# M5 of the last pass at the second level of Strassen-Winograd, with sums on VectorE and two fixed staging slots

## The chip, the cores and the metric

The kernel runs on one core of a Trainium2 chip. The metric is the device time of one execution in microseconds (us); lower is better. Engines that matter here: TensorE (PE in the profile; its weight loads are PEld), VectorE (DVE), ScalarE (ACT), GpSimd (POOL) and SyncE (SP), whose queue issues most of the transfers between the chip's main memory (DRAM) and the on-chip SBUF. Products accumulate in PSUM, eight banks of 512 fp32 columns.

## The reference, cut to what matters

```python
xn = layernorm(x)                               # x: 2048 x 1024
s  = linear_attention(xn, wqkv, 32 heads) @ wo
b  = (silu(xn @ w_gate) * (xn @ w_up)) @ w_down # 1024 -> 3584 -> 1024
out = x + s * silu(b)
```

Weights and activations are bf16. The change concerns the last of these products, `h @ w_down`, for the second half of the tokens that is worked on, and the write-out behind it.

## The kernel before, in words

The feed-forward part works in two passes of 1024 tokens. A pass first makes `h = silu(gate) * up`, [1024 x 3584] kept with the 3584 on partitions as 28 chunks of 128, in 28 steps (one weight block of gate or of up each), and then multiplies by `w_down`. Every product uses the Strassen-Winograd scheme: the operands are cut into 2x2 quarters, and seven products of quarters take the place of eight, with sums of quarters made before and after. For `h @ w_down` the quarters of `h` are A11, A12, A21, A22 (512 tokens x 14 chunks each); the products are M1 = A11 B11, M2 = A12 B21, M7 = S3 T3, M6 = S2 T2, M5 = S1 T1, M4 = A22 T4, M3 = S4 B22, in this order (`M_ORDER`), with S1 = A21+A22, S2 = S1-A11, S3 = A11-A21, S4 = A12-S2. M5 needs S1, written in place of A21.

In the last pass (`emit_down_m`, L1394) such a product is either done directly (`prod_t`, L1433: four token tiles, each 14 matmuls of 128x512), or cut once more by the same scheme ("second level", `l2_M`, L1469). The second level needs seven products of halves of tokens, chunks and columns: for each of two row halves 7 matmuls of 128x256. `L2 = (1, 2, 4)` says that M1, M2 and M4 are done so. It costs three kinds of preparation:

- *Sums of weights.* `l2_load` (L1102) loads a piece of the packed `w_down` from the DRAM tensors `wd`, `l2_sums` (L1134) makes four differences on GpSimd (L1144) and stores seven blocks to the DRAM tensor `l2_M` (L1145). This is done for M1 and M4 during the 28 steps of the last pass, in pieces of two chunk pairs (the fourth piece of each M is half as large): a load in every odd step (L1737), the differences a step later. M2's sums are made earlier by another way. Later `load_w` (L238) loads them from there.
- *Sums of activations* s1 to s4 (`l2_lhs`, L1160), chunk pair by chunk pair on GpSimd, 28 operations of 128x256 for each M. For M1 they lie in two slots of the weight ring (`r_spare`), for M2 and M4 in old tiles (`x_spare`).
- *Sums of results* on VectorE and ScalarE, in `l2_M`, with steps that let one M's products run while another's results are copied: a `yield` after the first two products, and a call of `fill()` ahead of product 4.

The weight ring (`w_slot`, L215) has 8 slots of 1 MB. All weights of the steps (`pk_g`, `pk_u`: one block a step), the staging pieces, `r_spare` and the weights of M1 to M3 go through it. `load_w_to(base + i + 5)` (L1697) asks for the block of step i+4, so five steps ahead at most. SyncE issues its transfers in an order that a planner lays down when the program is built; each transfer waits in that queue for what it needs (a free slot, a finished store), and what is queued behind it waits too. The order on the other four engines is the order of the program.

A step of the pass is `emit_a` of the next block (four products of 4 matmuls, L988 to L991) and `emit_b` of the current one (three, L1017 to L1019). 28 matmuls, all L966.

The write-out of a tile of results is `fin` (L1196): `y*s` (L1200), plus `x` (L1201), and a store (L1202). Its `x` and `s` come by `io_load` (L1184), one tile ahead of need in a pool `io` of five slots; the last three of the kernel go to the tiles S0, S1, S2 of the pool `sp`, which hold the sums of the activations of the gate and up products until the last `emit_a`. `k2` are small result tiles; `KA` and `KB` (L1538, L1545) hold running sums of results in fp32; `banks()` hands out four PSUM banks, in turn from two pools.

Of the kernel before, what the change touches and what calls it, by code (L numbers as in the profile page):

```python
# [21 lines left out]
def kernel(  # L22
# [165 lines left out]
    passes = list(range(NPASS - 1, -1, -1))  # L188
    NWA = NFG // 2
    M_ORDER = (1, 2, 7, 6, 5, 4, 3)  # L190
    L2 = (1, 2, 4)
    L2_ORDER = (1, 2, 5, 6, 7, 4, 3)
    NQ = NFG // 2
    CH = CW // 2
# [20 lines left out]
    def w_slot():  # L215
        return wgu.tile([P, 2, DC, FW], BF16, name="w_sb", tag="pk")
# [52 lines left out]
    def load_w_to(n):  # L269
        while w_next[0] < min(n, len(w_seq)):  # L270
            load_w()
# [680 lines left out]
    with ExitStack() as p3:  # L952
# [8 lines left out]
        def k2(shape, dt, name):  # L961
            return kp.tile(shape, dt, name=name, tag="k2")
# [135 lines left out]

        l2_q = deque((M, j) for M in L2 if M != 2 for j in range(0, NQ, 2))
        l2_live = deque()  # L1100

        def l2_load():  # L1102
            M, j0 = l2_q.popleft()
            kd, q = M_PACK[M]
            t = w_slot()
            v = t[:].rearrange("p h a b -> p (h a b)").rearrange("p (b j n) -> p b j n", b=8, n=CH)
            js = range(j0, min(j0 + 2, NQ))
            for j in js:
                for k, b0, b1 in ((0, 0, 7), (1, 1, 6)):
                    src = wd_drams[j][0 if kd == "a" else 1][:, k, q].rearrange("p (c n) -> p c n", n=CH)  # L1110
                    nc.sync.dma_start(out=v[:, b0:b1 + 1:b1 - b0, j - j0, :], in_=src)
            l2_live.append((M, js, v))
# [31 lines left out]
                nc.gpsimd.tensor_tensor(out=b(o_), in0=b(a_), in1=b(b_), op=ALU.subtract)  # L1144
            nc.gpsimd.dma_start(out=l2_drams[M][:, :, js.start:js.stop, :], in_=v[:, 0:7, 0:n_, :])  # L1145

        x_spare, r_spare = [], []

        def l2_bufs(M):
            v = [x[:].rearrange("p a b -> p (a b)").bitcast(F16) for x in x_spare]  # L1150
            if M == 1:
                v = [x[:].rearrange("p h a b -> p (h a b)").bitcast(F16) for x in r_spare]
            v = [x[:, 0:2 * NQ * 2 * P].rearrange("p (s j r n) -> p s j r n", s=2, j=NQ, r=2) for x in v]
            return [v[0][:, 0], v[0][:, 1], v[1][:, 0], v[1][:, 1]]

        def l2_quad(A, j):
            v = A[:, :, j].rearrange("p k (r t n) -> p k r t n", r=2, t=2)
            return v[:, 0, :, 0], v[:, 1, :, 0], v[:, 0, :, 1], v[:, 1, :, 1]

        def l2_lhs(M, A, j, eng):  # L1160
            a11, a12, a21, a22 = l2_quad(A, j)
            s1, s2, s3, s4 = [v[:, j] for v in l2_bufs(M)]
            eng.tensor_tensor(out=s1, in0=a21, in1=a22, op=ALU.add)
            eng.tensor_tensor(out=s2, in0=s1, in1=a11, op=ALU.subtract)
            eng.tensor_tensor(out=s3, in0=a11, in1=a21, op=ALU.subtract)
            eng.tensor_tensor(out=s4, in0=a12, in1=s2, op=ALU.subtract)

        def quads(h, a, t):
            return h[:].rearrange("p (j k a) t -> p k j a t", k=2, a=2)[:, :, :, a, t * TB:(t + 1) * TB]
# [14 lines left out]
        def io_load(after=None):  # L1184
            if not fq:
                return
            p, t, cc = key = fq.pop(0)
            r0 = p * TB2 + t * P
            pool, tg = (sp, "S%d" % len(fq)) if len(fq) < 3 else (iop, "io")
            io = pool.tile([P, 2, CW], BF16, name="io", tag=tg)  # L1190
            gate([nc.sync.dma_start(out=io[:, 0, :], in_=x2[r0:r0 + P, cc * CW:(cc + 1) * CW]),
                  nc.sync.dma_start(out=io[:, 1, :], in_=s_dram[r0:r0 + P, cc * CW:(cc + 1) * CW])],
                 after, sync=True)
            io_tiles[key] = io
# [199 lines left out]
        def emit_down_m(p, h, base):  # L1394
# [8 lines left out]
            def load(M, q=None):  # L1403

                n_ = max(i for i, key in enumerate(seq) if key[2][0] == M and q in (None, key[2][1])) + 1
                load_w_to(base + n_ + (NPK - 2 if M == 1 and q != 3 else NPK))

            def S3(k):
                return s3_[k // NWA][:, k % NWA]
# [7 lines left out]
            def tt(out, a, b_, op=ALU.add):  # L1417
                nc.vector.tensor_tensor(out=out, in0=a, in1=b_, op=op)
# [22 lines left out]
            def banks(n=TPB):  # L1441
                turn[0] += 1
                pool, tg = (pps, "s") if turn[0] % 2 else (ppm, "m")
                return [pool.tile([P, CW], FP32, name="dm", tag=tg)[:] for _ in range(n)]
# [24 lines left out]
            def l2_M(M, A, K, done, fill, in_place, dst=None):  # L1469
# [40 lines left out]
                for r in range(2):  # L1510
                    c0, c1 = c[r]
                    if K is None:
                        nc.scalar.copy(out=c1[:, lo], in_=zy[r][:, lo])
                    else:
                        tt(c1[:, lo], zy[r][:, lo], K[2 * r + 1][:, lo])
                        done(2 * r + 1, c1)
                    l2_p(M, 3, r, A, bk)
                    if in_place:
                        tt(c0, xw[r], K[2 * r])
                    else:  # L1520
                        tt(c0[:, hi], xw[r][:, hi], c0[:, hi])
                    if done is not None:
                        done(2 * r, c0)
# [13 lines left out]
            load_w_to(base + NPK - 2)  # L1537
            KA = kept("kA")  # L1538
            fins = deque()
            M7, M6, M5 = [], [], []  # L1540
            KB = []

            def fill7():
# [17 lines left out]
                flush(1)  # L1561
            load(7)
            sums(S4, A12, S2, ALU.subtract)
            for j in range(NQ):
                l2_lhs(4, quads(h, 1, 1), j, nc.gpsimd)
            M6 = banks()
            for t in range(TPB):
                prod_t(6, t, M6[t], True)
                tt(KB[t], M6[t], KB[t])
                tt(KA[t], M6[t], KA[t])  # L1570
            load(6)
            M5 = banks()
            for t in range(TPB):
                prod_t(5, t, M5[t], True)
                c = k2([P, CW], FP32, "c22")[:]
                tt(c, M5[t], KB[t])
                fins.append((t + TPB, 1, silu(c, "g22")))
                if len(fins) > 1:
                    flush(1)
            tt(KA[-1], M5[-1], KA[-1])  # L1580
            load(5)

            def out3(t):
                prod_t(3, t, M5[t], False)
                c = k2([P, CW], FP32, "c12")[:]
                tt(c, M5[t], KA[t])
                fins.append((t, 1, silu(c, "g12")))

            def done4(t, c):
                fins.append((t + TPB, 0, silu(c, "g21")))  # L1590

            def fill3():
                flush()
                out3(0)
            go(l2_M(4, quads(h, 1, 1), KB, done4, fill3, True))
            hs_ = [slice(0, 3 * CW // 4), slice(3 * CW // 4, CW)]
            out3(1)
            flush(len(fins) - 1)
# [15 lines left out]
        for pi, p in enumerate(passes):  # L1614
# [78 lines left out]
            for i in range(n):  # L1693
# [38 lines left out]
                if not first:  # L1732
                    if l2_live:
                        l2_sums()
                    if i in (17, 18):
                        r_spare.append(w_slot())
                    if i % 2 == 1 and l2_q:  # L1737
                        l2_load()
                    if i >= 18 and 4 * l2_j + 4 <= i:
                        l2_lhs(1, quads(h, 0, 0), l2_j, nc.gpsimd)  # L1740
                        l2_lhs(2, quads(h, 1, 0), l2_j, nc.gpsimd)
                        l2_j += 1
# [41 lines left out]
```

## Time and profile before

| What | us |
|---|---|
| median of 3 runs (lowest, highest) | 756.48 (756.29, 759.92) |
| the profiled execution | 756.18 |
| its span, first to last instruction | 754.4 |
| L966 matmuls of the last pass | to 668.9 |
| M1 begins (L1466) | 668.72 |
| M7, M6 and M5 in a row (L1430) | 693.14 to 726.5 |
| last matmul | 749.8 |
| last write-out addition on VectorE | 751.9 |
| GpSimd: differences for M1 and M4 (L1144), 32 operations | 526.1 to 616.0 |
| GpSimd: sums for M4 (in `l2_lhs`) | 684.4 to 715.5 |

The granted TensorE clock was 0.999 over the span. Times in the profile count from the first instruction. "Busy" is time in which an engine ran an instruction; matmuls overlap in the pipeline, so a single one has a length of 379 ns (width 512) or 273 ns (width 256), though the next starts sooner. The chain that ended last is followed back from the last instruction, at each step to what released it. In the lists of instructions a line has the start, the length, the engine, the line of the kernel, the operation, the tile written and the tile read; `x4` is a group of four.

### The profile page before, as it was taken

To read this page: it belongs to the slowest core of one execution; us is meant where nothing else is said; L and a number is where in the kernel's file an instruction comes from. 1 tells how busy PE (TensorE), PEld (TensorE's weight loads), DVE (VectorE), ACT (ScalarE), POOL (GpSimd) and SP (SyncE) were. 2 spreads that over 40 slices of the span, in tenths; PEclk is the share of its full clock that TensorE was granted. 3 is DMA by queue.
4 is the path that set the end of the run, shared out by engine and by line. 5 is a ranking of instruction groups with operands and counts; after the bars stand their busy time and mean duration, and the time that the engine had idled before them with its cause. 6 is when DMAs were issued, how large, how long until landed. Compare 5 with 4: busy or idle time off the path is not lost.

```text
span 754.4 us, 11075 instructions
## 1 busy us (share of the span) xinstructions
PE 745.8 (99%) x3857; PEld 360.8 (48%) x3857; DVE 581.4 (77%) x1040; ACT 381.1 (51%) x545; POOL 399.8 (53%) x500
## 2 busy tenths in 40 slices
PE   8999999999999999999999999999999999999997
PEld 3544444454454444444444444444444444467464
DVE  6687787887697788888889785468776877687966
ACT  5677776889956575656658311132323222232023
POOL 2444799998540266868585021811542569434900
PEclk9999999999999999999999999999999999999999
DMA  9967799879779668878799228789786768479652
GB/s 318 304 146 139 228 332 298 303 158 271 206 190 296 231 214 301 295 279 316 273 323 409 111 65 306 222 295 339 258 306 222 281 206 344 147 258 318 209 161 77
DMA packets 129160, 187.77 MB, mean 249 GB/s; under 512 B 36208, under 2 KB 104176, under 8 KB 119376
## 3 DMA queue, kind: packets, MB, share of 16 engines
q1 hardware_dynamic: 121760, 156.00, 63.9%
q0 software_dynamic: 5904, 28.58, 9.9%
q10 hardware_dynamic: 1440, 2.49, 1.1%
q8 instruction: 30, 0.49, 0.3%
q14 instruction: 26, 0.21, 0.1%
HBM read 119.47 MB, written 60.23 MB: 238 GB/s over the span
## 4 chain that ended last, share of the span: by engine, by line
PE 84%; DMA 7%; POOL 3%; DVE 2%; issue 2%; ACT 1%; SPq 1%; POOLq 0%; DVEq 0%; ACTq 0%
PE zw L966 19%; PE kv_ps L554 15%; PE xb L966 10%; PE q_ps L183 6%; PE dzw L1228 6%; PE dm L1430 6%; PE yb L966 5%; PE dm L1466 4%; PE dx L1228 3%; DMA l<-w_sb 3%; PE fx L816 3%; DMA w_sb<-wd 3%; PE s_ps L774 3%; POOL w_sb L1144 2%; PE dy L1228 2%
## 5 line engine op out<-in xcount | busy, mean ns | idle before, releaser
L966 PEld LDWEIGHTS <-w_sb 128*128 128x128 f16 (+1 forms) x1568 | 152.1, 98 | 183.8 <-DMA w_sb<-pk_u 1.3
L966 PE MATMUL xb<-xnT,w_sb 128*128 128x512 bf16 x448 | 115.0, 379 | 0.0
L554 PE MATMUL kv_ps<-wkv_sb,xnT 128*128 128x512 bf16 x512 | 113.7, 379 | 0.6 <-ACT xnT L543 0.4
L966 PE MATMUL zw<-xnT,w_sb 128*128 128x512 bf16 x448 | 105.8, 379 | 0.0
L966 PE MATMUL zw<-S,w_sb 128*128 128x512 f16 x448 | 105.8, 379 | 0.0
L321 POOL TENSOR_TENSOR w_sb<-w_sb 128x512 f16<-128x512 bf16 x42 | 50.2, 1195 | 95.7 <-DVE w_sb L309 51.3
L286 ACT ACTIVATE w_sb<-w_sb 128x2048 bf16<-128x2048 bf16 x42 | 79.9, 1902 | 3.9 <-DMA w_sb<-in_B_w_up_dram 3.9
L554 PEld LDWEIGHTS <-xnT 128*128 128x128 bf16 x512 | 48.3, 97 | 56.0 <-ACT xnT L543 0.8
L1144 POOL TENSOR_TENSOR w_sb<-w_sb 128x512 f16<-128x512 bf16 (+3 forms) x32 | 35.4, 1126 | 52.4 <-DMA w_sb<-wd 51.9
L1042 ACT ACTIVATE sg<-cg 128x1024 bf16<-128x1024 f32 x28 | 29.6, 1057 | 57.4 <-DVE cg L1035 57.4
L183 PE MATMUL q_ps<-xnT,wq_sb 128*128 128x512 bf16 x256 | 58.4, 379 | 0.0
L966 PE MATMUL yb<-S,w_sb 128*128 128x512 f16 x224 | 57.4, 379 | 0.8 <-DMA w_sb<-pk_u 0.8
L1035 DVE SCALAR_TENSOR_TENSOR cg<-zw,rc_all,s 128x1024 f32<-128x1024 f32 x28 | 35.9, 1284 | 25.3 <-PE zw L966 13.2
L994 DVE SCALAR_TENSOR_TENSOR s<-yb,rc_all,s 128x512 f32<-128x512 f32 x42 | 31.5, 749 | 27.3 <-ACT s L993 27.3
L322 POOL TENSOR_TENSOR w_sb<-w_sb 128x512 f16<-128x512 bf16 x42 | 50.5, 1202 | 3.3
L324 POOL TENSOR_TENSOR w_sb<-w_sb 128x512 f16<-128x512 bf16 x42 | 50.3, 1197 | 0.0
L323 POOL TENSOR_TENSOR w_sb<-w_sb 128x512 f16<-128x512 bf16 x42 | 50.2, 1196 | 0.0
L1202 POOL DMA_DIRECT2D out_dram<-io x16 | 8.9, 555 | 69.2 <-DVE io L1201 69.0
L993 ACT ACTIVATE s<-xb,rcl 128x512 f32<-128x512 f32 x14 | 9.6, 687 | 66.3 <-PE xb L966 66.3
L1228 PE MATMUL dx<-w_sb,hT 128*128 128x512 bf16 x112 | 42.4, 379 | 0.0
L993 ACT ACTIVATE s<-xb,rc_all 128x512 f32<-128x512 f32 x42 | 28.4, 676 | 22.0 <-issue 12.7
L309 DVE TENSOR_SCALAR w_sb<-w_sb,cs_all 128x2048 bf16<-128x2048 bf16 x35 | 36.7, 1048 | 2.8
(213 smaller groups left out, 1351.1 us busy)
## 6 DMA issues: line engine op xcount, KB each, us to landing
w_sb<-pk_g SPq DMA_DIRECT2D x27, 1024.0 KB, 6.6
pk_g<-w_sb SPq DMA_DIRECT2D x14, 1024.0 KB, 5.0
w_sb<-pk_u SPq DMA_DIRECT2D x14, 1024.0 KB, 8.3
pk_u<-w_sb POOLq DMA_DIRECT2D x13, 1024.0 KB, 5.8
w_sb<-l SPq DMA_DIRECT2D x9, 896.0 KB, 4.6
w_sb<-in_B_w_gate_dram SPq DMA_DIRECT2D x14, 512.0 KB, 6.4
w_sb<-in_B_w_down_dram SPq DMA_DIRECT2D x28, 256.0 KB, 4.8
w_sb<-in_B_w_up_dram SPq DMA_DIRECT2D x14, 512.0 KB, 5.4
```

The source lines that it names most:

```text
L183: nc.tensor.matmul(q_ps[:], lhsT=wq_sb[:, dc, g * P:(g + 1) * P], rhs=xn_ap(dc, btok), start=(dc == 0), stop=(dc == DC - 1))
L286: nc.scalar.activation(out=junk, in_=raw_view(key, t), func=ACT.Square, accum_out=asum[:])
L321: nc.gpsimd.tensor_tensor(out=T1, in0=b12, in1=b11, op=ALU.subtract)
L322: nc.gpsimd.tensor_tensor(out=T2, in0=b22, in1=T1, op=ALU.subtract)
L323: nc.gpsimd.tensor_tensor(out=T3, in0=b22, in1=b12, op=ALU.subtract)
L324: nc.gpsimd.tensor_tensor(out=T4, in0=b21, in1=T2, op=ALU.subtract)
L554: mm = nc.tensor.matmul(kv_ps[:], lhsT=xn_ap(dc, tok), rhs=wkv_sb[:, dc, c * CW:(c + 1) * CW], start=(dc == 0), stop=(dc == DC - 1))
L966: mm = nc.tensor.matmul(out, lhsT=lhs(k), rhs=rhs(k), start=(first and k == 0), stop=(k == HK - 1), skip_group_check=True)
L993: nc.scalar.activation(out=s1[:], in_=x_[:], func=ACT.Copy, scale=rc)
L1144: nc.gpsimd.tensor_tensor(out=b(o_), in0=b(a_), in1=b(b_), op=ALU.subtract)
L1228: nc.tensor.matmul(out, lhsT=lhs, rhs=rhs, start=first, stop=lastk, skip_group_check=True)
L1430: nc.tensor.matmul(out, lhsT=lhs_of(M)(k)[:, t * P:(t + 1) * P], rhs=w_of(M, k)[:, cols], start=first and k == 0, stop=k == NFG - 1, skip_ ...
```

## The change

M5 joins the products of the second level. Its sums of weights are four more staged pieces, so twelve in all. The staging no longer takes a ring slot for each piece: two slots are taken at step 3, and the pieces use them in turn, one piece in each of the steps 3 to 14. The same two slots later hold the sums of activations for M1 and then for M5, so the weights of M1, M2, M7, M6 and of the first three parts of M5 are asked for with six slots in the ring instead of eight. A new function makes the sums of activations for M5 and for M4 on VectorE, in eight operations of 7x128 columns each; for M4 they were 28 operations on GpSimd. M5's results go to fp32 tiles in S0 and S1, and are added from there; M3 gets banks of its own instead of accumulating onto M5's. All io tiles use the `io` pool. M5's first products stand ahead of M4's, and M4's first two fill M5's gap. The diff, cut to its core:

```diff
-    L2 = (1, 2, 4)
+    L2 = (1, 2, 4, 5)
...
         def l2_load():
             M, j0 = l2_q.popleft()
             kd, q = M_PACK[M]
-            t = w_slot()
+            while len(r_spare) < 2:
+                r_spare.append(w_slot())
+            t = r_spare[len(l2_q) % 2]
...
         def l2_bufs(M):
-            if M == 1:
+            if M in (1, 5):
                 v = [x[:].rearrange("p h a b -> p (h a b)").bitcast(F16) for x in r_spare]
...
+        def l2_lhs_all(M, A, eng):
+            sb = l2_bufs(M)
+            for r in range(2):
+                v = A.rearrange("p k j (r t n) -> p k j r t n", r=2, t=2)[:, :, :, r]
+                a11, a12, a21, a22 = v[:, 0, :, 0], v[:, 1, :, 0], v[:, 0, :, 1], v[:, 1, :, 1]
+                s1, s2, s3, s4 = [x[:, :, r] for x in sb]
+                eng.tensor_tensor(out=s1, in0=a21, in1=a22, op=ALU.add)
+                eng.tensor_tensor(out=s2, in0=s1, in1=a11, op=ALU.subtract)
+                eng.tensor_tensor(out=s3, in0=a11, in1=a21, op=ALU.subtract)
+                eng.tensor_tensor(out=s4, in0=a12, in1=s2, op=ALU.subtract)
...
-            pool, tg = (sp, "S%d" % len(fq)) if len(fq) < 3 else (iop, "io")
+            pool, tg = iop, "io"
...
-                load_w_to(base + n_ + (NPK - 2 if M == 1 and q != 3 else NPK))
+                load_w_to(base + n_ + (NPK - 2 if M in (1, 2, 7, 6, 5) and (M, q) != (5, 3) else NPK))
...
             sums(S4, A12, S2, ALU.subtract)
-            for j in range(NQ):
-                l2_lhs(4, quads(h, 1, 1), j, nc.gpsimd)
+            l2_lhs_all(5, quads(h, 0, 1).bitcast(F16), nc.vector)
             M6 = banks()
...
             load(6)
-            M5 = banks()
-            for t in range(TPB):
-                prod_t(5, t, M5[t], True)
-                c = k2([P, CW], FP32, "c22")[:]
-                tt(c, M5[t], KB[t])
-                fins.append((t + TPB, 1, silu(c, "g22")))
-                if len(fins) > 1:
-                    flush(1)
-            tt(KA[-1], M5[-1], KA[-1])
-            load(5)
+            l2_lhs_all(4, quads(h, 1, 1), nc.vector)
+            T5 = [sp.tile([P, 2, CW], FP32, name="kT", tag="S%d" % r) for r in range(2)]
+            T5 = [T5[t // 2][:, t % 2] for t in range(TPB)]
...
-                prod_t(3, t, M5[t], False)
+                prod_t(3, t, M3[t], True)
                 c = k2([P, CW], FP32, "c12")[:]
-                tt(c, M5[t], KA[t])
+                tt(c, M3[t], KA[t])
...
+            def done5(t, T):
+                c = k2([P, CW], FP32, "c22")[:]
+                tt(c, T, KB[t])
+                fins.append((t + TPB, 1, silu(c, "g22")))
+                tt(KA[t], T, KA[t])
+
+            M3 = []
+
             def fill3():
                 flush()
+                M3.extend(banks())
                 out3(0)
-            go(l2_M(4, quads(h, 1, 1), KB, done4, fill3, True))
+            m4_ = l2_M(4, quads(h, 1, 1), KB, done4, fill3, True)
+            go(l2_M(5, quads(h, 0, 1).bitcast(F16), None, done5, lambda: next(m4_), False, T5))
+            go(m4_)
...
-                    if i in (17, 18):
-                        r_spare.append(w_slot())
-                    if i % 2 == 1 and l2_q:
+                    if i >= 3 and l2_q:
                         l2_load()
```

In `l2_M` a call of `done` that stood in one branch now runs whenever `done` is given.

## The prediction

> **What bounds the kernel now.** I read, in this order: the page's busy table, the chain that ended last, the time line of SyncE's queue in the last pass, the waits of that queue, then VectorE's instructions in the last 90 us.
>
> ```profile
> PE 745.8 (99%) x3857; PEld 360.8 (48%) x3857; DVE 581.4 (77%) x1040; ACT 381.1 (51%) x545; POOL 399.8 (53%) x500
> ```
>
> TensorE is the bound: 745.8 of 754.4 us. A change pays only by shortening its stream, or loses by making it wait. The chain of work, around the two places that the change touches:
>
> ```profile
> 604.34 4.67 DMA l<-w_sb
> 609.05 2.17 DMA w_sb<-wd
> 615.04 0.90 POOL l L1145
> 618.67 5.10 DMA w_sb<-pk_u
> 623.81 1.04 PE yb L966 x4
> ...
> 668.88 18.34 PE dm L1466 x168
> 693.30 33.25 PE dm L1430 x154
> ```
>
> (start, length, what). Products of the second level (L1466, 128x256) come every 18.34/168 = 0.1092 us, those of the first (L1430, 128x512) every 33.25/154 = 0.2159. Ahead of them the chain runs through the staging of M1 and M4: a load from wd, four GpSimd differences, a store to `l2_M`, and behind it a weight load that TensorE waits for at 623.81 (the wait table gives that wait 0.8 us). So staging has no slack left even now. SyncE's queue shows why:
>
> ```profile
> 567.81 1.91 SPq L1111 DMA_DIRECT2D w_sb<-wd  x4
> 569.76 0.47 SPq L263 DMA_DIRECT2D w_sb<-pk_g  x1
> 570.27 0.43 SPq L263 DMA_DIRECT2D w_sb<-pk_u  x1
> 581.28 1.91 SPq L1111 DMA_DIRECT2D w_sb<-wd  x4
> 583.23 0.47 SPq L263 DMA_DIRECT2D w_sb<-pk_g  x1
> 583.74 0.43 SPq L263 DMA_DIRECT2D w_sb<-pk_u  x1
> 595.10 1.91 SPq L1111 DMA_DIRECT2D w_sb<-wd  x4
> 609.05 0.88 SPq L1111 DMA_DIRECT2D w_sb<-wd  x2
> ```
>
> ```profile
> SPq L1111 <- DMA l<-w_sb: 47.0, 5, 10.1
> ```
>
> Each staging load waits for the store of the piece before, and the gate/up weights of the next steps stand behind it in the queue. One turn (load, differences, store) takes 13.5, 13.8, 13.95 us.
>
> **Term 1, M5 on TensorE: -1.4.** Out: 4x14 products of 0.2159 = 12.09 us. In: 7 products x 2 row halves x 7 = 98 of 0.1092 = 10.70. All of it is on the path. The Trainium skill (TensorE: Matmul & The Clock Gate, section Back-to-back issue gap) speaks against this: it gives a sustained 131 ns at width 512 and 81 at 128, so by a straight line some 98 ns at 256 (an estimate), and M5 would become 2.3 us longer. This trace has 215.9 and 109.2 ns, and the trace decides.
>
> **Term 2, two waits that go: -0.8 and -0.3.** The 0.8 us at 623 came from slots taken from the ring at steps 17 and 18 just behind the last store; now they are taken at step 3. TensorE also waits 0.28 us at 728.35 for a ScalarE copy behind the g22 silus; in the new order that copy has M5's last products as cover. Bounds: 0 to -1.1.
>
> **Term 3, staging: +2.4 (0 to 9.7).** 12 pieces instead of 8, one each step (i = 3 to 14) instead of every second; two slots in turn, so the load of step i waits for the store of step i-2. Behind that wait in SyncE's queue stands the weight load of step i+5 (the keys up to 18 and 19 have to pass). A step is 28x0.2159 = 6.05 us. Key 21 would have begun at 623.0 without its wait, so key 18 begins at 623.0-3x6.05 = 604.85. The first load should start at 521.6, as now; five turns later step 13's four issues take 1.9 us, and key 18's weights land 6.0 us behind them (the pk_g load of 569.76 took 6.0). TensorE waits unless 521.6+5c+1.9+6.0 <= 604.85, that is unless a turn c of two pieces is at most 15.07 us. Low end for c: the DMA share in stages of 1 us from 567 to 582 sums to 10.1 us of all engines for two weights and one piece; weights alone move at 425 GB/s (511 to 517), 2.47 us each, so a piece is 5.1. Two weights and two pieces are 15.1, with a half piece 12.6; three of the five turns are of the first kind, mean 14.1, above the 13.7 of a turn alone. High end: the store of 538.15, the one that ran beside loads, took 8.0 us instead of 4.7, and 13.7+3.3 = 17.0. No row is nearer to two pieces at once than the one that made the high end, but it happened once, so I take the middle, 15.55: 5x(15.55-15.07) = 2.4; the ends give 0 and 9.7. GpSimd's own share, 4.6 to 5.3 us of differences and a 0.9 us issue a piece, fits into a step on average, since every fourth piece is half. VectorE is busy about 8.7 of 12.1 us in two steps there, which covers what GpSimd slows.
>
> **Term 4, two slots held longer: +0.3 (0 to 1.5).** M7's first weights were issued at 675.43 into the staging slot that M1 had just given back. Now the first free slot is M2's first, at 679.4, the second M1's third, at 681. M7's eight issues take some 0.63 us each and must have landed by 687.06 and 688.6, which they just do (last issue about 684.5, landing 2.4 to 6.1 us behind it). The M6, M5 and M4 loads have 5 us and more to spare.
>
> **VectorE: 0.** Its cover is the work that leaves GpSimd:
>
> ```profile
> L1418 DVE TENSOR_TENSOR hT<-hT x4: 684/686/1160, 683.0 to 684.8; 128x1024 f16<-128x1024 bf16 x4
> L1418 DVE TENSOR_TENSOR hT<-hT x3: 1151/1152/1160, 684.8 to 687.0; 128x1024 f16<-128x1024 bf16 x3
> ```
>
> The same operation (ns, min/median/max) takes 0.685 us alone and 1.15 from 684.4 on, when GpSimd computes M4's sums. With those moved off GpSimd, S2 (from 693.5) takes 4.3 us instead of 7.4, the four M7 evacuations with their fins end at 703.8, S4 at 708.1. An 896-wide sum is about 0.62 us, 0.57 in a row: eight for M5 end at 712.7, needed from 717.6 on. M6's evacuations follow, held by M6's end at 714.5, to 717.5; eight for M4 end at 722.1. Behind these is queued M5's `c1` addition, which must have read its bank before M5's last product at 726.8. Slack: 4.3 us. If the cover failed (all at the 1.15 rate), S4 would end at 716.6, then 7.1+4.8+7.1 us of sums and evacuations make 735.6, and M5's last product waits 9.3 us. M5's own extra additions (about 6 us, ending 732.2) end before M4's first, which waits for TensorE until 733.
>
> **Term 5, the end: +0.7 instead of the -1.7 of terms 1 and 2's second part.** The last three io tiles (x, s) were loaded from 661 to 664 into S0 to S2; M5's results now lie there, so they need slots that fins 9, 10 and 11 free. Fin 11's last addition ends at 746.9 now; it moves 1.7 earlier with TensorE and back by some 0.9, since fin 9 now waits for an io tile whose slot fin 8 frees, so 746.1. Then output landing 1.7, issue of two loads 0.8, landing 2.3, some 0.5 for outputs between them in the queue: 751.4, then 1.1 us of last additions: 752.5 against 751.9 now. So the path over io ends +0.6 to +0.7, the path over TensorE -1.7; the later counts. Ends: -1.7 (no io wait) and +3.8 (each of three loads behind the output before it, as at 723 to 738, where each pair costs 2.9 us).
>
> **Sum.** The profiled execution took 756.18 us, 1.8 more than its span; the median shown is 756.48, 0.3 more. 756.2 - 0.8 + 2.4 + 0.3 + 0.7 = 758.8. All ends low: 756.2-0.8-0.3-1.4 = 753.7.
>
> **Rivals.**
> - *Staging keeps pace* (c up to 15.1): term 3 is 0, and it is 756.4; without the io wait too, 753.7 to 754.5. For it: the low end of c, 14.1, and a planner that may put weights ahead of a staging load. Against it: the queue above kept key 14's load behind a staging load until 569.76 though its slot was free by 557.
> - *Staging is the bound*, the other side: one mechanism, the in-order queue at steps 11 to 14, where a staging load waits for a store and the weights of keys 16 to 19 wait behind it. It decides from a turn of 15.07 us; from 15.8 on the kernel is slower by over 0.5% (758.8 plus 1.2), at 17.0 it is 766.1.
> - *VectorE takes the bound* behind M6: 758.8+9.3 = 768, if the sums stay at 1.15 us a 1024 without GpSimd. The two rows above speak against it.
> - *It doesn't do what it says*: M5 gets no shorter, because its waits (copies, banks) eat 1.4 us. M1, M2 and M4 run without gaps at the same pace, so this is unlikely, and it would give 758.8 still, as the io path ends later.
>
> **Chances.** Staging keeps pace 0.38 (0.03 of it below 752.7 by luck of the measurement or a gain that I don't see), forecast 0.26 (turn 15.1 to 15.8), staging the bound 0.32, VectorE 0.04. 0.5% is 3.8 us, about what a measurement can tell from no change: faster 0.03, same 0.61, slower 0.36. The range, 753.7 to 765, leaves out the rest of the third case and the fourth.
>
> **What would show it.** M5's L1466 products at 0.109 us in a row; L1111 issues every 7 to 8 us from 521, and TensorE waiting for `w_sb<-pk` near 590 to 612 (if nowhere, term 3 is 0); VectorE's 896-wide sums at 0.6 us and M5's last product without a wait; io loads after 745 and a VectorE wait for DMA ahead of the last fins. The prediction is wrong if weights stand ahead of staging loads in the queue, if GpSimd isn't idle after 690, or if a wait appears in M5 or M4 that I have not named.

## The result and the profile after

The changed kernel takes 777.12 us (median of 4 runs, 776.89 to 778.36) against 756.38 for the kernel before in the same session (4 runs, 755.71 to 759.92): ratio 1.0268, 95% interval 1.0234 to 1.0301. I had forecast 758.8 with a range of 753.7 to 765.0, so the time lies 12 us outside. The profiled execution took 777.16 us, its span is 775.4.

Three marks cut the last 250 us of both profiled executions into parts: the end of the last L966 matmul (end of the 28 steps), the end of TensorE's last matmul, and VectorE's last addition.

| us | before | after | difference |
|---|---|---|---|
| steps end | 668.88 | 684.99 | +16.1 |
| down product (to the last matmul) | 80.91 | 82.91 | +2.0 |
| tail (to VectorE's last addition) | 2.10 | 4.64 | +2.5 |

The first line of the busy table is the one that answers to "PE 745.8 (99%)": TensorE is still the busiest, but no longer busy throughout.

```profile
PE 751.2 (97%) x3899; PEld 366.6 (47%) x3899; DVE 584.0 (75%) x1063; ACT 384.9 (50%) x557; POOL 394.3 (51%) x492
```

**The steps.** First TensorE's waits from 500 us on (total, times, longest), then its instructions that waited for weights (start, length, then in brackets the idle time ahead), then SyncE's queue around the first and the last of these:

```profile
PE yb L966 <- DMA w_sb<-pk_g: 12.0, 3, 6.5
PE dm L1478 <- ACT dm L1498: 2.0, 1, 2.0
```

```profile
586.03 1.89 PE L966 MATMUL yb<-S,w_sb 128*128 128x512 f16 x4 [5.12 <-DMA w_sb<-pk_g]
600.71 1.04 PE L966 MATMUL yb<-S,w_sb 128*128 128x512 f16 x4 [0.43 <-DMA w_sb<-pk_g]
619.46 1.89 PE L966 MATMUL yb<-S,w_sb 128*128 128x512 f16 x4 [6.49 <-DMA w_sb<-pk_g]
```

```profile
572.29 7.23 SPq L1114 DMA_DIRECT2D w_sb<-wd  x7
579.61 0.42 SPq L263 DMA_DIRECT2D w_sb<-pk_g  x1
580.08 0.42 SPq L1114 DMA_DIRECT2D w_sb<-wd  x1
580.59 0.42 SPq L263 DMA_DIRECT2D w_sb<-pk_u  x1
...
605.42 7.47 SPq L1114 DMA_DIRECT2D w_sb<-wd  x6
612.98 0.42 SPq L263 DMA_DIRECT2D w_sb<-pk_g  x1
```

L1114 is the staging load, L263 a weight load. A group of L1114 holds two pieces, which stand ahead of the pair of weights (a last single load in between belongs to a later piece): the first waits for the store of its slot, the second for that of the other slot, and only then come the weights, which land 6.4 us later (579.61 to 586.03) when TensorE has long stopped. The first loads of every second piece are issued at 522.01, 540.37, 556.90, 572.29, 591.23 and 605.42, so a turn takes 16.7 us on average. In the table of waits of SyncE's queue, the wait for stores (total, times, longest; 47.0 before) is now

```profile
SPq L1114 <- DMA l<-w_sb: 55.4, 7, 11.2
```

Behind the long waits TensorE is also slow. The same stretch in windows of 3 us, with the busy time of each engine, and then the granted clock, the DMA share and GB/s:

```profile
583.00:586.00 3.00, 0.00 (x0) 0.00 (x0) 0.00 (x0) 0.33 (x1) 2.63 (x4) 0.54 1.02 399
586.00:589.00 3.00, 2.97 (x8) 1.05 (x9) 0.00 (x0) 0.00 (x0) 2.44 (x4) 0.50 0.99 407
589.00:592.00 3.00, 3.00 (x13) 1.32 (x12) 1.07 (x2) 0.69 (x1) 0.00 (x0) 0.82 0.69 249
592.00:595.00 3.00, 3.00 (x16) 1.35 (x15) 2.57 (x4) 0.00 (x0) 0.00 (x0) 1.00 0.70 201
```

From 586 to 592 the clock is 0.50 and 0.82, and 21 matmuls fit where 28 belong. The first 16 matmuls behind the waits of 5.12 and 6.49 us took 5.45 and 5.79 us instead of 3.45, so each wait cost some 2.0 to 2.3 more.

**The down product.** M5's 98 products lie in the groups from 730.39 to 742.62, with 28 of M4 among them, and come at the pace of 0.109 us. What spoils the gain is the wait of 1.99 us in M4:

```profile
733.45 4.75 PE L1478 MATMUL dm<-w_sb 128*128 128x256 f16 x42
738.04 4.75 PE L1478 MATMUL dm<-w_sb,hT 128*128 128x256 f16 x42
742.62 1.69 PE L1478 MATMUL dm<-w_sb 128*128 128x256 f16 x14
744.15 3.22 PE L1478 MATMUL dm<-w_sb,kept 128*128 128x256 f16 x28
749.36 2.08 PE L1478 MATMUL dm<-w_sb,kept 128*128 128x256 f16 x14 [1.99 <-ACT dm L1498]
751.23 4.52 PE L1442 MATMUL dm<-w_sb,hT 128*128 128x512 bf16 x14
```

ScalarE's copy L1498 for M4 is queued behind M5's four `g22` silus, and these wait for VectorE's additions of M5. Behind the wait the clock is low too (14 matmuls in 4.52 us instead of 3.19).

VectorE did what I forecast: S4 (seven sums of 1024) in 4.30 us, 896-wide sums in 0.62 each.

```profile
719.91 4.30 DVE L1430 TENSOR_TENSOR hT<-hT 128x1024 f16<-128x1024 bf16 x7
724.12 0.62 DVE L1167 TENSOR_TENSOR w_sb<-hT 128x896 f16<-128x896 f16 x1
```

**The tail.** VectorE waits three times for io tiles at the end; the queue shows why the first comes late (L1214 a store of results, L1203 and L1204 the loads of `x` and `s`):

```profile
763.49 0.42 DVE L1212 TENSOR_TENSOR g<-g,io 128x512 bf16<-128x512 bf16 x1 [0.87 <-DMA io<-s_dram]
...
769.24 0.43 DVE L1212 TENSOR_TENSOR g<-g,io 128x512 bf16<-128x512 bf16 x1 [1.08 <-DMA io<-s_dram]
...
770.59 0.42 DVE L1212 TENSOR_TENSOR g<-g,io 128x512 bf16<-128x512 bf16 x1 [0.47 <-DMA io<-s_dram]
```

```profile
758.28 0.42 SPq L1214 DMA_DIRECT2D out_dram<-io  x1
760.84 0.33 SPq L1203 DMA_DIRECT2D io<-in_A_x_dram  x1
761.21 0.43 SPq L1204 DMA_DIRECT2D io<-s_dram  x1
```

### The profile page after: what moved, and what is told of

Its sections match the earlier page's. It is cut to its first block, busy times and chain, and to the rows that moved or that the text cites. A ratio compares the mean times of both kernels' runs of the same rounds, so it can differ in the third digit from the quotient of the medians.

```text
span 775.4 us, 11222 instructions
## 1 busy us (share of the span) xinstructions
PE 751.2 (97%) x3899; PEld 366.6 (47%) x3899; DVE 584.0 (75%) x1063; ACT 384.9 (50%) x557; POOL 394.3 (51%) x492
## 4 chain that ended last, share of the span: by engine, by line
PE 87%; DMA 6%; DVE 4%; ACT 1%; issue 1%; SPq 1%; POOL 0%; DVEq 0%; ACTq 0%
PE zw L966 23%; PE kv_ps L554 14%; PE xb L966 12%; PE q_ps L183 6%; PE yb L966 6%; PE dzw L1240 6%; PE dm L1478 4%; DMA w_sb<-pk_g 3%; PE dm L1442 3%; PE dx L1240 3%; PE s_ps L774 2%; PE fx L816 2%; PE dy L1240 1%; PE kvz L576 1%; PE nd L743 1%
## 5 line engine op out<-in xcount | busy, mean ns | idle before, releaser
L966 PEld LDWEIGHTS <-w_sb 128*128 128x128 f16 (+1 forms) x1568 | 153.0, 98 | 198.7 <-DMA w_sb<-pk_g 13.5
L966 PE MATMUL xb<-xnT,w_sb 128*128 128x512 bf16 x448 | 116.8, 384 | 0.0
L966 PE MATMUL zw<-S,w_sb 128*128 128x512 f16 x448 | 106.9, 382 | 0.0
L966 PE MATMUL zw<-xnT,w_sb 128*128 128x512 bf16 x448 | 105.8, 379 | 0.0
L966 PE MATMUL yb<-S,w_sb 128*128 128x512 f16 x224 | 59.2, 388 | 12.0 <-DMA w_sb<-pk_g 12.0
L1147 POOL TENSOR_TENSOR w_sb<-w_sb 128x512 f16<-128x512 f16 (+3 forms) x48 | 52.0, 1104 | 30.8 <-DMA w_sb<-wd 29.2
L1214 POOL DMA_DIRECT2D out_dram<-io x16 | 8.7, 544 | 74.0 <-DVE io L1213 73.5
```

Source lines behind the costliest of these rows:

```text
L966: mm = nc.tensor.matmul(out, lhsT=lhs(k), rhs=rhs(k), start=(first and k == 0), stop=(k == HK - 1), skip_group_check=True)
```

## The experiments

All times are medians beside runs of the kernel before on the same chip: 758.11 us (e1 to e4), 757.59 (e8 to e11), 757.65 (e12 to e15), 757.70 (e16, e17). The table has the three parts of the profiled executions.

| | us | ratio (95%) | steps end | down product | tail |
|---|---|---|---|---|---|
| e1 staging alone | 770.62 | 1.0168 (1.0138, 1.0197) | 682.10 | 80.91 | 2.09 |
| e2 down product alone | 764.80 | 1.0097 (1.0069, 1.0126) | 671.16 | 81.23 | 7.11 |
| e3 weights first | 767.05 | 1.0124 (1.0102, 1.0147) | 674.01 | 81.23 | 6.45 |
| e4 one difference | 776.09 | 1.0223 (1.0173, 1.0273) | 684.42 | 81.32 | 7.11 |
| e8 spread in the program | 782.62 | 1.0314 (1.0281, 1.0346) | 690.98 | 82.90 | 5.94 |
| e9 e8 + silus behind | 782.69 | 1.0332 (1.0297, 1.0366) | 689.38 | 79.09 | 7.11 |
| e10 e8 + two io tiles early | 780.50 | 1.0310 (1.0273, 1.0346) | 687.36 | 81.23 | 5.83 |
| e11 e8 + both | 777.67 | 1.0261 (1.0233, 1.0290) | 689.59 | 79.09 | 6.20 |
| e12 weights first + spread | 765.60 | 1.0108 (1.0075, 1.0142) | 668.04 | 87.31 | 6.04 |
| e13 M4's pieces a pass earlier | 773.53 | 1.0215 (1.0193, 1.0237) | 681.92 | 81.23 | 6.82 |
| e14 e13 + silus + io in two slots | 766.71 | 1.0122 (1.0099, 1.0146) | 679.83 | 79.09 | 2.09 |
| e15 e12 + silus + io in two slots | 758.84 | 1.0018 (1.0002, 1.0034) | 667.86 | 85.39 | 2.09 |
| e16 e15 + M2's sums early | 758.11 | 0.9986 (0.9966, 1.0006) | 667.85 | 84.02 | 2.10 |
| e17 e16 in 18 steps | 754.28 | 0.9954 (0.9940, 0.9968) | 667.96 | 79.28 | 2.10 |

### Which half of the change: e1 and e2

**e1**: the kernel before with the new staging only; M5's pieces are made and not used, M5 stays at the first level.

```diff
-        l2_q = deque((M, j) for M in L2 if M != 2 ...
+        l2_q = deque((M, j) for M in (1, 4, 5) ...
...
-            t = w_slot()
+            while len(r_spare) < 2:
+                r_spare.append(w_slot())
+            t = r_spare[len(l2_q) % 2]
...
-                    if i in (17, 18):
-                        r_spare.append(w_slot())
-                    if i % 2 == 1 and l2_q:
+                    if i >= 3 and l2_q:
```

> The changed staging alone: twelve pieces, two slots in turn, one a step from step 3 on, while the down product stays as before (M5 at the first level; its staged sums are stored and not read). Theory A (the loss in the steps is staging: weights stand in SyncE's queue behind staging loads that wait for stores, and TensorE's clock drops after each wait): TensorE waits some 12 us in the steps and loses some 4 us more to the lower clock, so 756.4+16-0.8 = about 772. Rival B (the loss comes from the new down product, or needs both): 756 to 758.

Measured 770.62. The steps end at 682.10 (+13.2), with waits for weights of 3.06 and 6.39 us; down product and tail are as before to 0.01 us. The staging alone costs 13.2 of the 16.1 us that the steps lost.

**e2**: the changed kernel with the old staging of 8 pieces; M5 multiplies by M4's staged weights, as its own are not made.

```diff
-for M in L2 if M != 2 for j
+for M in L2 if M not in (2, 5) for j
-            while len(r_spare) < 2: ...
+            t = w_slot()
-in_=l2_drams[M][...]
+in_=l2_drams[4 if M == 5 else M][...]
-                    if i >= 3 and l2_q:
+                    if i in (17, 18):
+                        r_spare.append(w_slot())
+                    if i % 2 == 1 and l2_q:
```

> The changed down product alone: staging of eight pieces as before; M5 runs at the second level with M4's staged weights in place of its own, so its weights are left out of the computation and its time is that of the change. Theory A: the steps end as before (668.9 us), the down product takes 2.0 us longer than before instead of 1.7 shorter (a wait of 2 us for a ScalarE copy, and the low clock behind it), the tail 2.5 us longer: 756.4+4.5 = about 761. Rival (the waits in the down product are an echo of the delayed steps): 755 to 757.

Measured 764.80, 6.7 us above the kernel before, where I expected 4.5. The down product is 0.3 longer than before instead of 1.7 shorter, with the 2.0 us wait for ScalarE in it, here without a drop of the clock; the tail is 5.0 longer. So the new down product has losses of its own, which have nothing to do with staging. The steps end 2.3 later than before, though the staging is that of before: waits for weights add up to 2.1 us instead of 0.8. What holds these weights up, and the rest of the 2.3, this run does not show; it may be what e1 lacks of the 16.1.

### Why the steps lost: e3, e4, e8, e12, e13

**e3**: the staging load of step i goes behind the weight load of block i+6 in SyncE's queue.

```diff
...
+                        load_w_to(base + i + (7 if i > 3 else 5))
-                        l2_load()
+                        l2_load(w_ins.get(keys[i + 6]) if i > 3 else None)
```

> The changed kernel, but the order of SyncE's queue is set: a staging load of step i stands behind the weight load of block i+6, so block n waits behind the piece of step n-7, where the changed kernel has it behind that of step n-4. Same bytes, same differences, same slots. Theory A (order of the queue): no wait for weights in the steps, 777.1-12.0-4.3 = about 761. Rival C (the DMA engines are too busy in these steps, share 0.9, to bring weights in time in any order): waits of 8 us or more remain, 770 to 777.

Measured 767.05, between the two expectations: of 12.0 us of waits one of 4.13 is left (at 621.21). The order is most of it (the edit also asks for the weights two blocks earlier, which this order needs; the two are not separated). But the turn has grown to 18.4 us, so in this order the twelve pieces do not fit into the steps 3 to 14 beside the weights.

**e4**: three of the four GpSimd differences left out from the third piece on.

```diff
-            for o_, a_, b_ in ((2, 7, 0), (3, 6, 2), (4, 6, 7), (5, 1, 3)):
+            for o_, a_, b_ in (...)[0:4 if M == 1 and js.start < 4 else 1]:
```

> The changed kernel with one of the four GpSimd differences of each piece from the third on (three are left out of the computation; loads and stores as in the changed kernel): GpSimd's part of a turn falls from 4.6 to some 1.2 us. If a turn is the sum of its parts (load, differences, store), it falls from 16.7 to some 13.5 us and the waits in the steps go: about 761. If a turn is set by the bytes (15.1 us of all DMA engines for two weights and two pieces), it stays at 15 to 16.5 us and 5 us or more of waiting remain: 766 to 774.

Measured 776.09 (769.18 to 777.49), waits of 0.31, 4.34, 1.90 and 4.22 us. GpSimd's share of a turn fell by 3.4 us, the turn from 16.7 to 15.1 (first loads from 523.18 to 598.50; from the third piece on, which is where the edit begins, from 16.3 to 14.1). So the differences are part of a turn. But with a turn at the prediction's limit of 15.07 us, 10.8 us of waits are left, where the sum of term 3, started at 523.18, gives some 1.5: the turn alone does not decide. The planner's order of the queue changed as well, so more than that this run does not tell.

**e8**: the pieces in 12 of the steps 1 to 21, M1's sums in steps 23 to 25.

```diff
-                    if i >= 3 and l2_q:
+                    if i in (1, 3, 5, 7, 8, 10, 12, 14, 15, 17, 19, 21):
...
-                        l2_lhs(1, quads(h, 0, 0), l2_j, nc.gpsimd)
+                    if 23 <= i < 26:
+                        l2_lhs(1, quads(h, 0, 0), 2 * (i - 23), nc.gpsimd)
+                        l2_lhs(1, quads(h, 0, 0), 2 * (i - 23) + 1, nc.gpsimd)
```

> The changed kernel, with the 12 staging pieces spread over steps 1 to 21 (1, 3, 5, 7, 8, 10, 12, 14, 15, 17, 19, 21) instead of one each step from 3 to 14; M1's sums on GpSimd, which overwrite the two staging slots, move from steps 18 to 24 to steps 23 to 25. Same bytes, same slots, same instructions. Theory A (the 12 us of waits for gate/up weights and the low clock behind them come of asking for 12 pieces in some 95 us, so that the DMA engines are full and the weights stand in line): waits for pk_g and pk_u sum to under 1.5 us, the steps end (start of the down product) at 668 to 670 instead of 685, the down product takes 81.2, the tail 5 to 7, total 760 to 763. Theory B (the bytes or the in-order queue as such, whatever the pace): waits of 4 us and more remain, steps end after 676, total 768 or more.

Measured 782.62, waits of 15.7 us: worse. Taken at its word my theory fell here, but the queue shows that nothing had been spread:

```profile
598.12 2.92 SPq L1114 DMA_DIRECT2D w_sb<-wd  x6
601.14 0.42 SPq L263 DMA_DIRECT2D w_sb<-pk_g  x1
601.64 0.38 SPq L263 DMA_DIRECT2D w_sb<-pk_u  x1
612.72 7.33 SPq L1114 DMA_DIRECT2D w_sb<-wd  x6
620.14 0.42 SPq L263 DMA_DIRECT2D w_sb<-pk_g  x1
```

Still two pieces ahead of each pair of weights, and the last at 612.72. The place of a load in the program does not set its place in the queue; the planner does.

**e12**: the spread of e8, held by e3's order.

```diff
...
                     if i in (1, 3, 5, 7, 8, 10, 12, 14, 15, 17, 19, 21):
+                        load_w_to(base + i + (7 if i > 3 else 5))
-                        l2_load()
+                        l2_load(w_ins.get(keys[i + 6]) if i > 3 else None)
```

> e8 failed to spread anything: the planner put the staging loads two and two ahead of the weights all the same. Here the same spread (steps 1 to 21) is enforced: the staging load of step i (from 5 on) goes behind the weight load of block i+6 in SyncE's queue, as in e3. Same bytes, slots and instructions as the changed kernel. Theory A (12 pieces in some 95 us fill the DMA engines, and the weights behind them come late): now the weights are never behind a piece that is not yet due, and the pieces have 110 us: waits for weights under 1.5 us in all, steps end at 668 to 671 instead of 685, down product 81.2, tail 5 to 7, total 760 to 763. Theory B (the pieces cost this whatever their order and pace): waits of 4 us and more, steps end after 675, total 766 or more.

Measured 765.60, but the steps are what this run is for: they end at 668.04, 16.9 us earlier than in the changed kernel and 0.8 earlier than before, with the same pieces, bytes and slots. No wait for weights is left. SyncE's queue, and all that TensorE waited for from 400 us on:

```profile
566.69 1.92 SPq L1116 DMA_DIRECT2D w_sb<-wd  x4
568.71 0.41 SPq L264 DMA_DIRECT2D w_sb<-pk_u  x1
569.22 0.38 SPq L264 DMA_DIRECT2D w_sb<-pk_g  x1
569.70 3.55 SPq L1116 DMA_DIRECT2D w_sb<-wd  x4
574.84 0.33 SPq L264 DMA_DIRECT2D w_sb<-pk_u  x1
```

```profile
PE dm L1480 <- POOL w_sb L1177: 2.5, 1, 2.5
PE dm L1480 <- ACT dm L1500: 2.0, 1, 2.0
PE dm L1444 <- issue: 0.2, 1, 0.2
```

Pieces and weights now alternate. What keeps the total up, beside the 2.0 us wait for ScalarE (with low clock behind it here) and the tail, is a loss that e12 makes itself: M1's sums, moved to the last steps, end too late on GpSimd (2.5 us, and low clock behind it).

**e13**: M4's pieces made in the pass before from weight tiles that lie in SBUF, as M2's are; 8 pieces are left in the steps, in the old way.

```diff
+                    if fresh and not last and st % 2 == 1:
+                        if st // 2 < NQ:
+                            l2_early(4, st // 2, False)
+                        if 0 <= st // 2 - 2 < NQ:
+                            l2_early(4, st // 2 - 2, True)
...
```

> All four second-level products, but M4's operand pieces are made in the pass before, from the weight tiles that lie in SBUF there (as M2's are, in the second half of the b stage), so that only 8 pieces (M1, M5) are loaded, summed and stored during the steps, one every second step in ring slots, at the pace of the kernel before. The complete computation. Theory A (number of pieces per time): steps end at 669 to 671 (as in e2, which also stages 8), down product 81.2, tail 6 to 7: total 763 to 765. Rival: the extra stores of 3.2 MB around 490 to 520, where the DMA engines were 83 to 100% busy, delay the first weights of the last pass: steps end later than 673, total 767 or more.

Measured 773.53: the loss that the rival forecast, but not by the bytes it named. M4's stores (L1127) wait in SyncE's queue for GpSimd's differences (11.4 us in all from 485 to 515) and stand between the first weights of the last pass; the first of these is issued at 504.33, where the kernel before issued it at 494.32, and TensorE waits 8.24 us for it. From 490 to 505 the DMA engines were less busy (0.67) than before (0.83). So transfers that wait hold up the weights once more, in the queue or in ring slots that such tiles still occupy, rather than a lack of DMA time:

```profile
510.11 1.89 PE L966 MATMUL yb<-S,w_sb 128*128 128x512 f16 x4 [8.24 <-DMA w_sb<-pk_u]
```

```profile
500.62 0.37 SPq L1127 DMA_DIRECT2D l<-w_sb  x1
503.85 0.37 SPq L1127 DMA_DIRECT2D l<-w_sb  x1
504.33 0.45 SPq L263 DMA_DIRECT2D w_sb<-pk_u  x1
```

### Why the down product and the tail lost: e9, e10, e11, e14, e15

**e9**: M5's silus issued behind M4's copies.

```diff
             def done5(t, T):
-                c = k2([P, CW], FP32, "c22")[:]
-                tt(c, T, KB[t])
-                fins.append((t + TPB, 1, silu(c, "g22")))
                 tt(KA[t], T, KA[t])
+                tt(T, T, KB[t])
+                late5.append((t, T))
...
             def fill3():
+                for t, T in late5:
+                    fins.append((t + TPB, 1, silu(T, "g22")))
                 flush()
```

> e8 with M5's four g22 silus issued on ScalarE behind M4's copies instead of ahead of them. If the 2.0 us wait of TensorE in M4 is ScalarE's in-order queue: the wait is gone, the down product takes 79.2 to 79.5 (1.4 less than before the change). But the end is set by the io tiles (theory: three tiles that wait for slots freed by earlier outputs), so the tail grows by what TensorE gains: total 760 to 762, within 0.7 of e8. Rival (TensorE still sets the end): total 2 below e8.

The wait is gone and the down product takes 79.09 us, 1.8 less than before the change, as expected; e11 and e14 give the same 79.09. The medians of e8 and e9 are alike (782.62 and 782.69), but their executions spread over 5 us and more (779.39 to 784.48, 780.21 to 786.03), so that shows little. By the parts, down product and tail together are 2.6 shorter than in e8, of which 1.7 are low clock that e8 had behind the wait. Against e2, without that low clock, the down product is 2.1 shorter and the tail the same (7.11): the tail did not grow by what TensorE gained, though I had expected that. (The total of 760 to 762 rested on the steps that I had expected of e8.)

**e10** and **e11**: the last two io tiles in S2, which M5's results leave free, without and with e9's edit.

```diff
...
-            pool, tg = iop, "io"
-            io = pool.tile([P, 2, CW], BF16, name="io", tag=tg)
+            if len(fq) < 2:
+                if not io2:
+                    io2.append(sp.tile([P, 2, 2, CW], BF16, name="io", tag="S2"))
+                io = io2[0][:, len(fq)]
+            else:
+                io = iop.tile([P, 2, CW], BF16, name="io", tag="io")
```

> e8 with the last two io tiles in the third of the freed S buffers, which M5's results leave unused, loaded early as before the change. If the tail is the io tiles' slots: VectorE's waits for DMA at the end go, tail 2.1, the down product stays at 81.2, total 756 to 757.5. Rival (the tail comes from VectorE's late additions behind M5's): tail stays over 4 us, total 759 or more.

> e8 with both edits, silus behind and two io tiles early. If all three losses are the ones named: steps end 668 to 670, down product 79.2 to 79.5, tail 2.1 to 2.5: total 754 to 756, the M5 gain of 1.4 at last visible, that is 0.1 to 0.3% below the kernel before. If something else binds: 757 or more.

Tails of 5.83 and 6.20 us: wrong. The wait that counts is the first (2.50 us in e10, 3.03 in e11), and the last two tiles are not in it. By the code, `fill3` puts the write-out of M3's first tile ahead of M4's four, while its io tile is the fifth in the order of loads; it takes the slot that M5's last write-out gives back. Output at 758.28, load at 760.84, addition at 763.49 in the changed kernel: the times fit.

**e14**: e13, with e9's edit and all seven io tiles that are still due at the end of M5 in the two slots of M5's sums, behind M3's weights in the queue.

```diff
             go(l2_M(5, ...))
+            for i in range(min(len(fq), 8)):
+                v = r_spare[i // 4][:].rearrange("p h a b -> p (h a b)")
+                io_load(w_ins[0], v=v[:, (i % 4) * 2 * CW:(i % 4 + 1) * 2 * CW]...)
             go(m4_)
```

> e13 with M5's g22 silus behind M4's copies on ScalarE, and with all the io tiles that are still to be loaded when M5 ends put into the two ring slots that held M5's sums, issued at once behind M3's weights. e10 and e11 showed that the last two tiles alone do not help: the first wait is for a tile further ahead. If the tail is the io tiles' slots as a chain (5 tiles, each reloaded when its output has left): VectorE's waits for io at the end go, tail 2.1 to 2.6, down product 79.1 as in e9: total 754.5 to 757, so level with the kernel before or 0.2% ahead. Rival: tail stays above 4 us, total 759 or more.

Measured 766.71, since e13's wait is still in it; but the down product takes 79.09 and the tail 2.09, as it was before the change. VectorE has no wait for io tiles left. That shows that the tail came from the io tiles: from their slots, or from the place of their loads in the queue, both of which this edit changes.

**e15**: e12 with the same two edits.

> e12 with the two edits of e14 (silus behind, io tiles in the two slots of M5's sums). Down product 79.1, tail 2.1 to 2.6 whatever the steps do; with e12's steps by theory A (668 to 671) total 754 to 757; by theory B 760 or more.

Measured 758.84. Steps and tail as expected; the down product has the 3.2 us for GpSimd, and low clock behind it.

### Is that all: e16 and e17

**e16**: e15 with M2's sums from step 6 on (`i >= 6`). **e17**: the pieces in steps 1 to 19 as well, M1's sums one a step from 21 on.

```diff
-                    if i in (1, 3, 5, 7, 8, 10, 12, 14, 15, 17, 19, 21):
+                    if i in (1, 3, 5, 7, 8, 10, 11, 13, 14, 16, 18, 19):
...
-                    if i >= 18 and 4 * l2_j + 4 <= i:
+                    if i >= 6 and 4 * l2_j + 4 <= i:
...
-                    if 23 <= i < 26:
+                    if 21 <= i < 27:
+                        l2_lhs(1, quads(h, 0, 0), i - 21, nc.gpsimd)
```

> e15, with M2's sums on GpSimd as soon as their quadrants are there (from step 8 on) instead of from step 18 on. e12 and e15 had no wait for weights, but a new one: M1's sums, which e12 had moved to steps 23 to 25, came 3.2 us late on GpSimd behind M2's, with about 3 us of low clock behind that. Theory A (that wait was the last loss, and the 12 pieces cost nothing once they are spread and in order): M1's sums end by about 670, the wait is under 0.5 us, steps end at 668, down product 79.1 to 79.8, tail 2.1, span 752 to 752.7, total 753.5 to 754.7, that is 0.3 to 0.5% below the kernel before. Rival (there is a further cost of the pieces that the wait hid, such as late second-level weights): total 756 or more.

> e16 with the 12 pieces in steps 1 to 19 instead of 1 to 21, and M1's sums one quadrant a step from step 21 on. It asks how much slack the pace of e12 has: 12 pieces in 18 steps (109 us) instead of 20 (121 us). By the bytes (about 54 us of all engines for the pieces and 2.47 for each of 18 weights, 98 us) it should still fit: no wait for weights, total as e16 or up to 0.5 lower. If pieces have to come at one per 10 us or slower: a wait of 2 to 4 us comes back between 560 and 610, total 757 or more.

e16 missed its point: its M1 sums still begin at 653.65, since they wait for the store of the last piece out of their slot, not for M2's sums; the wait stays at 3.2 us (758.11). Of its twelve executions four took 753.6 to 754.6 us, as e17's do, the rest 756.5 to 759.5; the profile is of one of the long ones, and why the four were shorter is not shown. e17 ends the staging earlier, M1's sums begin at 642.08, and TensorE waits for nothing from 500 us on. It takes 754.28 us, ratio 0.9954 (0.9940 to 0.9968): faster than both kernels. Its busy line, the down product at its beginning and M5:

```profile
PE 744.6 (99%) x3899; PEld 365.1 (49%) x3899; DVE 583.8 (78%) x1063; ACT 384.6 (51%) x557; POOL 393.5 (52%) x492
```

```profile
667.79 3.22 PE L1479 MATMUL dm<-w_sb,hT 128*128 128x256 bf16 x28
670.85 4.75 PE L1479 MATMUL dm<-w_sb 128*128 128x256 f16 x42
...
716.42 4.75 PE L1479 MATMUL dm<-w_sb 128*128 128x256 f16 x42
```

Against the profiled run of before, VectorE's last addition is 2.55 us earlier: 0.9 in the steps (the old wait at 623 is gone) and 1.6 in the down product. So in this arrangement nothing else of the change costs time, and the staging of twelve pieces is free when it is spread and stands behind the weights: the DMA engines are 0.84 to 0.99 busy in each 15 us from 520 to 640, and no weight is late.

## Why the prediction was wrong, point by point

The profiled execution came out 18.4 us above the forecast. Three steps make 18.0 of it.

- **Term 3, staging: this failed.** The mechanism and the place were right (TensorE waits for key 18's weights behind a staging load that waits for a store), the size was not. I put key 18's weights at 521.6+5c+1.9+6.0, 607.25 with c = 15.55 and 2.4 us late; they came at 619.46, which is 14.6 late. Of the 12.2 us between, 5.7 are the order of the queue: I assumed the weights behind one piece ("step 13's four issues take 1.9 us"), where the planner put two pieces ahead of them, and the second waited for its own slot's store (605.42 to 612.98, 7.56 us). Another 5.7 are the turn, 16.7 us instead of 15.55, near the high end that I had worked out. The rest is start and landing, 0.4 and 0.5. The order was my worst assumption: I named as a danger that weights might stand *ahead* of staging loads, and never the reverse; e3 and e12 show that it decides, and e4, where a turn of 15.1 us left 10.8 us of waits.
- **A term that was missing: TensorE's clock.** A wait of 6.49 us cost 2.3 more behind it. Together, 14.6+2.3-0.8 (the old wait, which did go as term 2 says) is the 16.1 of the steps. I had seen 0.999 before, where TensorE hardly ever stops, and did not ask what happens once it does. The Trainium skill (TensorE: Matmul & The Clock Gate, section Part 1: The HAM clock gate) says that the clock falls to half after an idle window of some 3.4 us and recovers after a busy one, and that this window runs freely. The rows agree with the half (0.50), and with chance in it: behind the same wait of 2.0 us in M4 the clock dropped in the changed kernel, e8 and e12, and not in e2, e3, e4, e10 and e13. They do not agree with the length: waits of 2.0 and 2.5 us, shorter than that window, were enough.
- **Terms 2 and 5, the down product and the end: 3.5 us.** I gave the `g22` silus M5's last products as cover and looked at M5's copies only; M4's copies, now close behind, are queued after the same silus: the 2.0 us wait that e9 takes away, and in this run 1.7 of low clock. Term 5's mechanism was right (e14, e15), and its rows were the ones I named (io loads late, VectorE waiting), but it was mis-sized: I put it at 2.4 us (+0.7 instead of -1.7), and between e9 and e14 the tail falls by 5.0 (7.11 to 2.09). Most of that is the first of the waits: 0.9 us in my chain, 3.04 in e2. In e2, where the clock does not drop, down product and tail together are 5.3 longer than before, and I had 1.0 (0.7, and term 4's 0.3): 2.1 of the difference are this wait, 2.0 ScalarE's.
- **Term 1, M5 at the second level: right.** 98 products at 0.109 us; the down product is 1.8 shorter once its wait is gone (terms 1 and 2 said 1.7). The two sustained figures of the skill's section on the issue gap, by which I worked out +2.3, are not borne out by any run here.
- **Term 4: too high.** I took +0.3; with 79.09 nothing of it is seen.
- **VectorE: right**, within 0.1 us in each sum, and no product of M5 waited for it.
- **Rivals.** The outcome is "staging is the bound", on the far side of its high end, 766.1. The chance of 0.36 for slower was too low: with the turn of 15.07 us as the point of decision and rows of 14.1 and 17.0 around it, a middle of 15.55 already lay beyond it, and I knew nothing against the high end but that its row came once.

Open remains how the turn of 16.7 us divides between GpSimd's differences, the bytes and the order of transfers: e4, meant for it, changed the queue as well.

## What to carry to other kernels

When a transfer that waits is put into an in-order queue, read the order from the planned queue, not from the program, and count everything that stands between the wait and the next load that TensorE needs; then pace the added transfers (e17: twelve in 18 steps and behind the weights cost nothing, in 12 steps and ahead of them 16 us). An engine's wait of several microseconds costs more than its length if it stops TensorE. A faster product pays only if what is behind it (copies on ScalarE, slots for the write-out) keeps up: here the whole gain of 1.8 us was lost until both were moved.

## What the runs showed of the hardware

- Behind waits of 2.5 us and more (e12, e15, e16, the changed kernel) TensorE's clock was 0.50 to 0.61 in windows of 3 us and took 3 to 6 us of work to recover: 1.4 to 2.7 us lost each time. Waits of 2.0 us went either way, and behind waits of 1.7 to 1.9 us (e4, e9, e13) it stayed at 1.00.
- With GpSimd idle, VectorE's 1024-wide sum in 16 bits took 0.61 us in a row of seven, with GpSimd at work 1.15 (the rows of before). Moving sums from GpSimd to VectorE was thus no burden for VectorE.
- DMA engines that are 0.84 to 0.99 busy for 120 us (e17) made TensorE wait for no weights; in the changed kernel the share was lower while the weights stood in the queue behind waiting loads (0.59 and 0.82 from 571 to 583, 0.65 from 607 to 613), and TensorE waited all the same. The share alone does not tell.
